# A fused transformer block: low parts of turned attention results on GpSimd, ScalarE's statistics a slot later, two more residual blocks turned by DMA

## The chip, the cores and the metric

The kernel runs on one core of a Trainium2 chip. The core has five engines that each work through a list of instructions of their own: TensorE (PE; its weight loads are shown apart as PEld), VectorE (DVE), ScalarE (ACT), GpSimd (POOL) and SyncE (SP), which here only issues DMAs. The metric is the device time of one execution in microseconds (us). The kernel before takes 512.64 us, the median of three runs (511.61 to 512.82).

## What is computed

One pre-norm transformer block over 2048 tokens of 512 features: sliding, dilated attention (32 heads of 16 features, 8 keys per query, 2 tokens apart), then a layer with 1792 hidden units and a squared ReLU. All in float32.

```python
h  = x + attention(layernorm(x) @ wqkv) @ wo
h2 = h + relu(layernorm(h) @ w1 + b1)**2 @ w2 + b2
```

where, for each query position, the attention is

```python
idx    = pos[:, None] - arange(8) * 2
logits = einsum("bhsd,bhswd->bhsw", q, k[idx]) * scale      # masked where idx < 0
o      = einsum("bhsw,bhswd->bhsd", softmax(logits), v[idx])
```

## The kernel before

**Blocks and groups.** The 2048 tokens are 16 *blocks* of 128 tokens, t = 0 to 15, and four blocks make a *group* (group 0 is blocks 0 to 3, group 1 blocks 4 to 7 and so on). A block fills the 128 partitions.

**High and low parts.** TensorE multiplies in a shortened float32 (`F32R`). To keep the precision, each operand is split in two: the high part is a copy to that type, made on ScalarE (`hi`, L147), the low part is the operand less its high part, a subtraction on VectorE or GpSimd (`lo`, L150). A product is then three products: high by high, low by high, high by low (`mm3`, L232). Names ending in h and l are such parts: `oh` and `ol` of an attention result, `rh` and `rl` of a hidden unit's result, `big_l` (in one of its uses) of the turned residual.

**Stages.** First the products with wqkv (L232, tiles mm), group by group; their results go through memory (`qkv_d`), and the attention reads windows of them back. Then, for each group, the output product with wo (tiles wo), the norm, the first layer of the MLP (L232 again) and the second one (L870, tiles acc). The MLP of the first three groups (u = 0, 1, 2) runs while the blocks of the next group are prepared, and the products with wo of that next group stand in between. The last group's MLP has a schedule of its own (L793).

**Attention** runs beside all this on VectorE and GpSimd, as a stream of small steps: a product of q with a window of k (L343, pr<-qp,k), a reduction (L377, ex<-pr), a softmax over 8 keys, and a *weighing*, the product of the softmax with a window of v (L354, pr<-ex,v). The weighing is added up over the keys by three additions on GpSimd (L411: 256, 128 and 64 wide per row, here called one set of *sums*), the last of which writes the attention result o.

**Slots.** The order of all instructions is written by hand: the program goes through *slots* (one slot is one step of products on TensorE), and `at(n, ...)` puts a piece of work n slots on, `after(n, ...)` behind the attention steps of that slot. At the end of a slot the `at` pieces are issued, then `pump` issues as many attention steps as a running count of VectorE's time allows (`now["dve"]`, advanced by `dve(...)`, against TensorE's `now["pe"]`), then the `after` pieces. So a piece that no longer counts for VectorE also lets attention steps be issued earlier. Engines take what is issued to them in that order; buffers and results are guarded by semaphores.

**A block on its way from attention to the MLP.** The result o of a block has to be turned (features onto partitions) before the product with wo; so has the normed residual hn before the MLP. Either TensorE does it (four transposes, L205, into a tile tr), or a DMA: blocks 4, 5, 8, 9, 12 and 13 (the tables `OV` and `HV`) are turned by DMA. Then `o_split` copies o into two planes of 16 bits on ScalarE (L594, pl<-o), `turn_dma` issues a transposing DMA on SP (L598), and two slots after the split `o_join` puts the planes together again on ScalarE (L603), makes the high part oh (L147) and, at the end of that slot, the low part ol (`lo_T`, L150, on VectorE). The product with wo (`wo_product`) follows at the start of the next slot. For these six blocks its order is wo_h by oh, wo_l by oh, and last wo_h by ol (`lows_last`), four instructions each.

When the product is done, `h_add` (L639) adds the residual on VectorE: h<-wo,h. It then takes the statistics of the norm: for blocks 4, 5, 8, 9, 12 and 13 (`AS`) on ScalarE (`act_stats`, L181 to L183, tiles scrap, nm and sq), for the others on VectorE. GpSimd finishes them (L187 to L190), `h_norm` (L200) applies them on ScalarE, and hn is turned like o.

```python
        hi_T(tr, [oT[t][0]])
        after(0, lo_T, tr, [oT[t][0]], [oT[t][1]])
```

(o_join's last two lines: the high part on ScalarE, then the low part.)

Of the kernel before, what the change touches and what calls it, by code (L numbers as in the profile page):

```python
# [19 lines left out]
R = 4  # L20
RI = 2
# [9 lines left out]
LAG = 3  # L31
AS = (4, 5, 8, 9, 12, 13)
OV = (4, 5, 8, 9, 12, 13)
HV = (4, 5, 8, 9, 12, 13)
SLOW = 1.01, 1.10, 1.06
DELAY = 3
WJ = 2
# [1 line left out]
OT = 4, 5, 10, 12  # L39
WO = 7, 9, 13, 15  # L40
HT = 20, 20, 21, 23
OK = (-6, -2, 4), (-5, -1, 5), (3, 6, 10), (4, 7, 12)
HK = (12, 15, 18), (14, 16, 19)
W2 = (18,)
LH = 3, 4, 10, 11
OP = 6, 7, 12, 13
# [12 lines left out]
def block_kernel(ctx, tc, x, wqkv, wo, w1, b1, w2, b2, out):  # L59
# [52 lines left out]
    def at(delta, fn, *a):  # L112
        due.setdefault(now["slot"] + delta, []).append((fn, a))

    def after(delta, fn, *a):
        late.setdefault(now["slot"] + delta, []).append((fn, a))
# [14 lines left out]
    def dve(t):  # L131
        now["dve"] += t
# [16 lines left out]
    def lo(eng, dst, src, h):  # L149
        eng.tensor_tensor(out=dst, in0=src, in1=h, op=ALU.subtract)  # L150
# [63 lines left out]
        for d, src in parts(tr, h_dst):  # L214
            hi(d, src)

    def lo_T(tr, h_dst, l_dst):
        for (d, src), h in zip(parts(tr, l_dst), h_dst):
            lo(nc.vector, d, src, h)
            dve(0.16 + 0.53 / len(h_dst))  # L220

    def mm3(ps, lh, ll, rh, rl, mid=None, at_=2 * KB, lows_last=False):

# [346 lines left out]
    def o_T(t):  # L570
        s, j = divmod(t, RI)
        pump(until=s)
        tr = transposes(o_t[s][:, j, :])
        if t % R == RI:

            ohl = att.tile([P, 2, KB, P], F32R, name="ohl", tag="o", bufs=3)
            oT[t] = ohl[:, 0], ohl[:, 1]
        else:
            oT[t] = row("oh", (P, KB, P), F32R), row("ol", (P, KB, P), F32R)
        at(0, hi_T, tr, [oT[t][0]])  # L580
        at(0, lo_T, tr, [oT[t][0]], [oT[t][1]])
# [30 lines left out]
    def o_join(t):  # L612
        turn_join(("o", t))
        tr = planes.pop(("o", t))
        if t % R == RI:
            ohl = att.tile([P, 2, KB, P], F32R, name="ohl", tag="o", bufs=3)
            oT[t] = ohl[:, 0], ohl[:, 1]
        else:
            oT[t] = row("oh", (P, KB, P), F32R), row("ol", (P, KB, P), F32R)
        hi_T(tr, [oT[t][0]])  # L620
        after(0, lo_T, tr, [oT[t][0]], [oT[t][1]])

    def h_split(t):
        turn_split(("h", t), hn.pop(t))
# [12 lines left out]
    def h_add(t, ps):  # L637
        h = hs[t]
        nc.vector.tensor_tensor(out=h, in0=ps, in1=h, op=ALU.add)  # L639
        dve(0.7)  # L640
        (act_stats if t in AS else norm_stats)(t, h)

    def h_norm(t):
        hn[t] = row("hn")
# [13 lines left out]
    def wo_product(t, slots):  # L658
        ps = turn["mm"].tile("wo")
        oh, ol = oT.pop(t)  # L660
        mm3(ps, lambda k: oh[:, k, :], lambda k: ol[:, k, :],
            lambda k: wo_h[:, k, :], lambda k: wo_l[:, k, :], lows_last=t in OV)
        for n, (fn, a) in zip(slots, ((h_add, (t, ps)), (h_norm, (t,)), (add_b2, (t,)),
                                      (spill, (t,)))):
            (after if fn in (h_norm, spill) else at)(n + (fn is add_b2), fn, *a)

# [311 lines left out]
    def first_phase(t0):  # L980
        def chores(m):
            if t0 + 3 < 16:
                if m in (0, 2):
                    at(0, x_stats, t0 + 2 + m // 2)

                early = t0 == 12
                if m + early in (6, 7):
                    at(0, x_norm, t0 - 4 + m + early)
                if m in XT[early]:
                    x_T(t0 + 2 + XT[early].index(m))  # L990
            if t0 + 5 < 16 and m in (6, 9):
                at(0, load_x, t0 + 2 + m // 3)
            if jobs and m % 3 == 0:
                at(0, weight_job)
            k = t0 // 2 * 12 - 72 + m
            if k == 19:
                dve(HOLD)
            for t in range(R):
                if k == OT[t]:
                    at(0, load_h, t)  # L1000
                    if t not in OV:
                        o_T(t)
                if t in OV and k in OK[t]:
                    at(0, (o_split, lambda t: turn_dma(("o", t)), o_join)[OK[t].index(k)], t)
                if t in HV and k in HK[t]:
                    at(0, (h_split, lambda t: turn_dma(("h", t)),
                           lambda t: turn_join(("h", t)))[HK[t].index(k)], t)
                if k == WO[t]:
                    wo_product(t, (1, 3, 4, 6))
                    now["pe"] += 2.73  # L1010
                if k == HT[t]:
                    (at(0, h_parts, t) if t in HV else h_T(t))
            if k in W2:
                at(0, load_w2, W2.index(k))

        def half(m):
            end_slot(1.37)
            chores(m)

        for n in range(6):  # L1020
            chores(2 * n)
            qkv_of(t0 + n % 2, n // 2, lambda: half(2 * n + 1))
            end_slot(1.37)
# [41 lines left out]
    for u in range(R - 1):  # L1065
        now["sub"] = u
        first, end = u == 0, False
        fs = list(range(FB)) if first else [*sorted(place), 12, 13]
        fs += [f for f in range(12) if f not in fs and (u < 2 or f not in ENDS)]
        fs += ENDS if u == 2 else []  # L1070
        need = [] if first else [f for f in fs if f < 12 and f not in place]
        acc = [psum.tile([P, D], F32, name="acc", tag=tag) for tag in ("acc0", "acc1", "tr0", "tr1")]
        js = range(R)


        todo, halves = {}, {}
        for i in js:
            t = R * (u + 1) + i
            if not end:
                a = i // 2 if u == 2 else 0  # L1080
                o0 = OP[i] - a
                if t in OV:
                    turned = [(o0, at, 0, o_split, t), (o0, after, 0, turn_dma, ("o", t)),
                              (o0 + 2, at, 0, o_join, t)]
                else:
                    turned = [(o0, o_T, t)]
                if t in HV:
                    h0 = 12
                    turned += [(h0, at, 0, h_split, t), (h0, after, 0, turn_dma, ("h", t)),
                               (h0 + 2, at, 0, turn_join, ("h", t))]  # L1090
                for p, *what in ((LH[i] - a, at, 0, load_h, t), *turned,
                                 (WP[i] - a, wo_product, t, (0, 1, 2 + 3 * a, 3 + 3 * a))):
                    todo.setdefault(p, []).append(what)
                p, h = (HP[i], i % 2) if u < 2 else HL[i]
                if t in HV:
                    todo.setdefault(p, []).append((at, 0, h_parts, t))
                else:
                    (todo, halves)[h].setdefault(p, []).append((h_T, t))
            todo.setdefault(UP[i], []).append((at, 0, unspill, R * u + i))
        if u == 2:  # L1100
            for p, *what in ((12, at, 0, t_load, 0), (12, at, 0, t_load, 1), (13, after, 0, t_sums, 0),
                             (13, after, 0, t_sums, 1), (13, at, 1, t_split, 0),
                             (14, after, 0, t_split, 1)):
                todo.setdefault(p, []).append(what)

        def half(p):
            run(due)
            for fn, *a in halves[p]:
                fn(*a)

        for p in range(FB + LAG):
            more = 0.0
            if p == FB:
                run(due)
                dve(HOLD)
            if u < 2 and p == FB - 2:
                dve(HOLD)
            for fn, *a in sorted(todo.get(p, []), key=lambda x: x[0] is wo_product):
                fn(*a)
                more += 2.73 if fn is wo_product else 0.0  # L1120
            if p < FB:
                mlp1(u, fs[p])
                more += 2.73
                if first:
                    at(0, split_w2, p)
                    if p + 1 < FB:
                        load_w2(p + 1)
            q = p - LAG
            if q >= 0:
                f = fs[q]  # L1130
                mlp2(u, f, acc, js, q == 0, q == FB - 1,
                     (lambda: half(p)) if p in halves else None)
                more += 2.74
                if f < 12 and (need or first and p < FB - LAG):
                    free.append(place.pop(f))
                    if need:
                        at(1, fetch, need.pop(0))
            end_slot(more)
        for i in js:
            at(u // 2, finish, R * u + i, acc[i])  # L1140
# [83 lines left out]
```

## Time and profile before

| what | value |
|---|---|
| median of 3 runs | 512.64 us (511.61 to 512.82) |
| the profiled execution | 512.31 us, of which span 510.5 us |
| granted TensorE clock, mean | 0.999 |

The span is the time from the first to the last instruction. Busy time of the engines by stretch, from the view by windows (us):

| stretch | PE | DVE | ACT | POOL | what runs |
|---|---|---|---|---|---|
| 0 to 64 | 60.10 | 45.91 | 31.71 | 34.32 | start, products with wqkv of group 0 |
| 64 to 160 | 96.00 | 87.94 | 59.70 | 77.34 | products with wqkv, wo of group 0 |
| 160 to 260 | 100.00 | 87.32 | 62.82 | 76.34 | MLP of group 0, wo of group 1 |
| 260 to 360 | 98.83 | 87.48 | 54.62 | 78.43 | MLP of group 1, wo of group 2 |
| 360 to 430 | 70.00 | 32.92 | 40.64 | 48.74 | MLP of group 2, wo of group 3 |
| 430 to 510.5 | 76.92 | 35.16 | 41.40 | 36.08 | MLP of group 3 |

In the rows of the profile that follow, a group of instructions reads: line, engine, operation, tile written <- tiles read, shape, count | busy time, mean ns of one | idle time of the engine before them, and what ended it. A row of a timeline begins with the start and the duration in us, and ends, where the engine stood idle, with that idle time and what ended it. Rows of the chain of waits have start, duration, engine and tile.

### The profile page before, as it was taken

The numbers are of one execution on the slowest core, as the hardware profiler recorded it, in microseconds if no ns is written. First come the engines' busy times: TensorE is split into PE (matmuls) and PEld (weight loads), VectorE is DVE, ScalarE is ACT, GpSimd is POOL, SyncE is SP. The second block draws the span as 40 slices with busy tenths as digits, with TensorE's granted clock in tenths as the row PEclk, the third lists the DMA queues.
The fourth block names the chain that finished last, engine by engine and source line by source line (L and its number), as shares of the span: only waits on it lengthen the run. The fifth ranks groups of instructions, "written<-read, shape, count | busy, mean of one in ns | idle before, by whom it ended". The sixth has DMA issues, their size and how long they took to land. (4 is left out here: it accounts for less than half of the span.)

```text
span 510.5 us, 7598 instructions
## 1 busy us (share of the span) xinstructions
PE 501.9 (98%) x2460; PEld 424.4 (83%) x2460; DVE 376.7 (74%) x512; ACT 290.9 (57%) x552; POOL 351.2 (69%) x430
## 2 busy tenths in 40 slices
PE   7999999999999999999999999999999999999997
PEld 6999788888888888888888878888888888998986
DVE  5479899988998899788879979899963046832233
ACT  4634686767434767485364557264564737666541
POOL 4714799895786798786778768776897364685610
PEclk9999999999999999999999999999999999999999
DMA  8678998989677889666587955767672172444112
GB/s 264 180 225 203 256 295 299 271 285 274 204 225 214 276 301 272 200 199 174 182 253 217 226 166 163 202 199 249 207 152 67 52 217 84 160 142 133 62 42 83
DMA packets 100912, 100.52 MB, mean 197 GB/s; under 512 B 21000, under 2 KB 69384, under 8 KB 100872
## 3 DMA queue, kind: packets, MB, share of 16 engines
q1 hardware_dynamic: 99928, 99.52, 65.4%
q10 hardware_dynamic: 944, 0.52, 0.3%
q8 instruction: 19, 0.31, 0.3%
q14 instruction: 21, 0.17, 0.1%
HBM read 72.65 MB, written 24.25 MB: 190 GB/s over the span
## 5 line engine op out<-in xcount | busy, mean ns | idle before, releaser
L411 POOL TENSOR_TENSOR pr<-pr 128x512 f32<-128x512 f32 (+1 forms) x128 | 132.5, 1035 | 45.7 <-DVE pr L354 40.3
L232 PE MATMUL mm<-big_l,w_h 128*128 128x512 f32 x336 | 88.7, 390 | 0.0
L354 DVE TENSOR_TENSOR pr<-ex,v 128x1024 f32<-128x1024 f32 x64 | 78.2, 1222 | 12.8 <-POOL o L411 6.5
L343 DVE TENSOR_TENSOR pr<-qp,k 128x1024 f32<-128x1024 f32 x64 | 76.9, 1202 | 5.6 <-ACT qp L272 5.5
L377 DVE TENSOR_REDUCE ex<-pr 128x64 f32<-128x1024 f32 x64 | 78.4, 1226 | 1.9
L232 PEld LDWEIGHTS mm<-big_l,w_h 128*128 128x128 f32 x336 | 62.8, 188 | 13.0
L150 POOL TENSOR_TENSOR rl<-r,rh 128x512 fp32r<-128x512 f32 x42 | 56.2, 1339 | 19.6 <-ACT rh L147 16.5
L232 PE MATMUL mm<-big_h,xl 128*128 128x512 f32 (+1 forms) x208 | 56.0, 379 | 0.2 <-DVE xl L150 0.2
L232 PE MATMUL mm<-big_h,xh 128*128 128x512 f32 (+1 forms) x208 | 53.5, 378 | 0.7 <-ACT xh L147 0.7
L232 PE MATMUL mm<-big_l,xh 128*128 128x512 f32 (+1 forms) x208 | 52.8, 375 | 0.0
L870 PE MATMUL acc<-big_l,rh 128*128 128x512 f32 x190 | 52.2, 390 | 0.0
L870 PE MATMUL acc<-big_h,rh 128*128 128x512 f32 x190 | 52.1, 391 | 0.0
L501 ACT COPY y<-mm 128x512 f32<-128x512 f32 (+1 forms) x52 | 28.6, 552 | 41.2 <-PE mm L232 33.0
L870 PE MATMUL acc<-big_h,rl 128*128 128x512 f32 x190 | 51.7, 389 | 0.0
L846 ACT ACTIVATE r<-mm,b_sb 128x512 f32<-128x512 f32 x42 | 28.8, 685 | 32.4 <-PE mm L232 32.3
L232 PE MATMUL mm<-big_l,w_l 128*128 128x512 f32 x168 | 45.0, 389 | 0.0
L232 PEld LDWEIGHTS mm<-big_h,xh 128*128 128x128 f32 x208 | 37.6, 188 | 7.0 <-ACT xh L147 1.5
L232 PEld LDWEIGHTS mm<-big_l,xh 128*128 128x128 f32 x208 | 38.2, 188 | 6.1 <-POOL big_l L150 0.2
L232 PEld LDWEIGHTS mm<-big_h,xl 128*128 128x128 f32 x208 | 37.2, 188 | 5.8 <-DVE xl L150 0.6
L870 PEld LDWEIGHTS acc<-big_h,rl 128*128 128x128 f32 x190 | 35.7, 188 | 7.5
L870 PEld LDWEIGHTS acc<-big_l,rh 128*128 128x128 f32 x190 | 35.5, 188 | 7.4
L870 PEld LDWEIGHTS acc<-big_h,rh 128*128 128x128 f32 x190 | 34.9, 188 | 6.7
(160 smaller groups left out, 904.1 us busy)
## 6 DMA issues: line engine op xcount, KB each, us to landing
k<-qkv_d SPq DMA_DIRECT2D x48, 288.0 KB, 2.8
v<-qkv_d SPq DMA_DIRECT2D x48, 288.0 KB, 3.2
qkv_d<-y SPq DMA_DIRECT2D x18, 512.0 KB, 4.2
big_l<-w2l_d SPq DMA_DIRECT2D x24, 256.0 KB, 3.0
xt<-in_A_x_dram SPq DMA_DIRECT2D x16, 256.0 KB, 4.6
q<-qkv_d SPq DMA_DIRECT2D x32, 128.0 KB, 4.7
h<-in_A_x_dram SPq DMA_DIRECT2D x16, 256.0 KB, 3.9
h_d<-h SPq DMA_DIRECT2D x16, 256.0 KB, 3.2
```

Source lines behind the costliest of these rows:

```text
L150: eng.tensor_tensor(out=dst, in0=src, in1=h, op=ALU.subtract)
L232: nc.tensor.matmul(ps, l(k), r(k), start=(n == 0), stop=(n == 3 * KB - 1))
L343: nc.vector.tensor_tensor(out=pr.rearrange("p i w h d -> p i w (h d)"), in0=qps["now"][:, j % 2].unsqueeze(2).to_broadcast([P, RI, W, GC]) ...
L354: nc.vector.tensor_tensor(out=p2, in1=vwin, op=ALU.mult, in0=e1[:, :, :, j * GH:(j + 1) * GH].unsqueeze(4).to_broadcast([P, RI, W, GH, DH]))
L377: nc.vector.tensor_reduce(out=lf[:, :, :, j * GH:(j + 1) * GH], in_=pr, axis=X, op=ALU.add)
L411: nc.gpsimd.tensor_tensor(out=dst, in0=p2[:, :, :w], in1=p2[:, :, w:2 * w], op=ALU.add)
L501: nc.scalar.copy(y[:, :, t % RI * GC:(t % RI + 1) * GC], ps[:, :j * GC].rearrange("p (j c) -> p j c", j=j))
L846: nc.scalar.activation(r, ps, AF.Relu, bias=b1_sb[:, f:f + 1])
L870: nc.tensor.matmul(acc[j], l[:, j * P:(j + 1) * P], w[f], start=(first and n < len(js)), stop=(last and n >= len(terms) - len(js)))
```

## The change

Four edits, in one diff:

1. `act_stats` is issued one slot after `h_add` instead of in its slot, and `h_norm` of those blocks follows at the slot after that, ahead of the attention steps instead of behind the ones of the slot before.
2. The low part ol of a block turned by DMA is made by GpSimd instead of VectorE, with no time counted for VectorE. For blocks 12 and 13 it is issued ahead of the slot's attention steps instead of behind them.
3. Blocks 0 and 1 join `HV`: their normed residual is turned by DMA in the stage of the products with wqkv (split at step 12 or 14 of its count, join at 18 or 19), and not by TensorE at step 20.
4. The table entries for turning o in group 0 by DMA go away (`OK`; no block of group 0 was in `OV`). The new terms in `o0` and `turned` apply to blocks with `i >= RI`, and no such block is in `OV`, so they move nothing.

```diff
-HV = (4, 5, 8, 9, 12, 13)
+HV = (0, 1, 4, 5, 8, 9, 12, 13)
...
-OK = (-6, -2, 4), (-5, -1, 5), (3, 6, 10), (4, 7, 12)
-HK = (12, 15, 18), (14, 16, 19)
+HK = (12, 18), (14, 19)
...
-    def lo_T(tr, h_dst, l_dst):
+    def lo_T(tr, h_dst, l_dst, eng=nc.vector):
         for (d, src), h in zip(parts(tr, l_dst), h_dst):
-            lo(nc.vector, d, src, h)
-            dve(0.16 + 0.53 / len(h_dst))
+            lo(eng, d, src, h)
+            if eng is nc.vector:
+                dve(0.16 + 0.53 / len(h_dst))
...
         hi_T(tr, [oT[t][0]])
-        after(0, lo_T, tr, [oT[t][0]], [oT[t][1]])
+        (after if t < 3 * R else at)(0, lo_T, tr, [oT[t][0]], [oT[t][1]], nc.gpsimd)
...
         dve(0.7)
-        (act_stats if t in AS else norm_stats)(t, h)
+        if t in AS:
+            at(1, act_stats, t, h)
+        else:
+            norm_stats(t, h)
...
-            (after if fn in (h_norm, spill) else at)(n + (fn is add_b2), fn, *a)
+            more = fn is add_b2 or fn is h_norm and t in AS
+            (after if fn in (h_norm, spill) and not (fn is h_norm and t in AS) else at)(
+                n + more, fn, *a)
...
-                    if t not in OV:
-                        o_T(t)
-                if t in OV and k in OK[t]:
-                    at(0, (o_split, lambda t: turn_dma(("o", t)), o_join)[OK[t].index(k)], t)
-                if t in HV and k in HK[t]:
-                    at(0, (h_split, lambda t: turn_dma(("h", t)),
-                           lambda t: turn_join(("h", t)))[HK[t].index(k)], t)
+                    o_T(t)
+                if t in HV and k == HK[t][0]:
+                    at(0, h_split, t)
+                    after(0, turn_dma, ("h", t))
+                if t in HV and k == HK[t][1]:
+                    at(0, turn_join, ("h", t))
...
-                o0 = OP[i] - a
+                o0 = OP[i] - a - (2 if i >= RI and t in OV else 0)
                 if t in OV:
-                    turned = [(o0, at, 0, o_split, t), (o0, after, 0, turn_dma, ("o", t)),
+                    turned = [(o0, at, 0, o_split, t), (o0, at if i >= RI else after, i // RI, turn_dma, ("o", t)),
                               (o0 + 2, at, 0, o_join, t)]
```

How the built order moves, at three places. The numbers behind the names are the program's own and differ a little between the two builds; no time is in these rows.

VectorE around h_add of block 4 (h_2101 before, h_2095 now), before:

```order
L354 TENSOR_TENSOR pr_2390<-ex_226,v_2234 128x1024
L377 TENSOR_REDUCE ex_226<-pr_2343 128x16x4
L343 TENSOR_TENSOR pr_2400<-qp_2398,k_2336 128x1024
L354 TENSOR_TENSOR pr_2406<-ex_226,v_2284 128x1024
L150 TENSOR_TENSOR ol_2385<-pl_2271,oh_2384 128x512
L150 TENSOR_TENSOR big_l_85<-raw2_2306,big_h_84 128x512
L639 TENSOR_TENSOR h_2101<-wo_2412,h_2101 128x512
L377 TENSOR_REDUCE ex_226<-pr_2400 128x16x4
```

and now:

```order
L354 TENSOR_TENSOR pr_2388<-ex_226,v_2271 128x1024
L377 TENSOR_REDUCE ex_226<-pr_2341 128x16x4
L343 TENSOR_TENSOR pr_2398<-qp_2396,k_2334 128x1024
L149 TENSOR_TENSOR big_l_85<-raw2_2299,big_h_84 128x512
L639 TENSOR_TENSOR h_2095<-wo_2406,h_2095 128x512
L354 TENSOR_TENSOR pr_2460<-ex_226,v_2282 128x1024
L377 TENSOR_REDUCE ex_226<-pr_2398 128x16x4
L343 TENSOR_TENSOR pr_2468<-qp_2396,k_2343 128x1024
L354 TENSOR_TENSOR pr_2472<-ex_226,v_2390 128x1024
```

The low part is gone from VectorE, and the weighing that stood ahead of h_add (pr_2406) now stands behind it (pr_2460).

GpSimd between the low parts of blocks 4 and 5, before (neither is here):

```order
L411 TENSOR_TENSOR pr_2390<-pr_2390 128x2x256
L411 TENSOR_TENSOR pr_2390<-pr_2390 128x2x128
L411 TENSOR_TENSOR o_2113<-pr_2390 128x2x64
L150 TENSOR_TENSOR rl_2454<-r_2452,rh_2453 128x512
L411 TENSOR_TENSOR pr_2406<-pr_2406 128x2x256
L411 TENSOR_TENSOR pr_2406<-pr_2406 128x2x128
L411 TENSOR_TENSOR o_2113<-pr_2406 128x2x64
L411 TENSOR_TENSOR pr_2481<-pr_2481 128x2x256
```

and now, with ol_2383 of block 4 and ol_2455 of block 5:

```order
L411 TENSOR_TENSOR o_2111<-pr_2388 128x2x64
L149 TENSOR_TENSOR ol_2383<-pl_2265,oh_2382 128x512
L149 TENSOR_TENSOR rl_2448<-r_2446,rh_2447 128x512
L411 TENSOR_TENSOR pr_2460<-pr_2460 128x2x256
L411 TENSOR_TENSOR pr_2460<-pr_2460 128x2x128
L411 TENSOR_TENSOR o_2111<-pr_2460 128x2x64
L411 TENSOR_TENSOR pr_2472<-pr_2472 128x2x256
L411 TENSOR_TENSOR pr_2472<-pr_2472 128x2x128
L411 TENSOR_TENSOR o_2111<-pr_2472 128x2x64
L149 TENSOR_TENSOR ol_2455<-pl_2320,oh_2454 128x512
```

Each low part stands behind the sums of its slot; between the two are the sums of two weighings, pr_2460 and pr_2472, both issued by VectorE behind h_add of block 4. Blocks 8 and 9 read the same way.

GpSimd at the end of the attention, by blocks 12 and 13, before:

```order
L411 TENSOR_TENSOR pr_4197<-pr_4197 128x2x256
L411 TENSOR_TENSOR pr_4197<-pr_4197 128x2x128
L411 TENSOR_TENSOR o_3988<-pr_4197 128x2x64
L150 TENSOR_TENSOR rl_4235<-r_4233,rh_4234 128x512
L411 TENSOR_TENSOR pr_4202<-pr_4202 128x2x256
L411 TENSOR_TENSOR pr_4202<-pr_4202 128x2x128
L411 TENSOR_TENSOR o_3988<-pr_4202 128x2x64
L150 TENSOR_TENSOR rl_4288<-r_4286,rh_4287 128x512
```

and now:

```order
L411 TENSOR_TENSOR o_3986<-pr_4195 128x2x64
L411 TENSOR_TENSOR pr_4200<-pr_4200 128x2x256
L411 TENSOR_TENSOR pr_4200<-pr_4200 128x2x128
L411 TENSOR_TENSOR o_3986<-pr_4200 128x2x64
L149 TENSOR_TENSOR rl_4236<-r_4234,rh_4235 128x512
L149 TENSOR_TENSOR ol_4242<-pl_4127,oh_4241 128x512
L149 TENSOR_TENSOR rl_4286<-r_4284,rh_4285 128x512
L149 TENSOR_TENSOR ol_4292<-pl_4185,oh_4291 128x512
```

The last set of sums has moved ahead of rl, and the two low parts, of blocks 12 and 13, stand behind it, one rl apart.

## The prediction

> **What bounds the kernel now.** I read the page's first part, then TensorE's list of waits, then the chain of waits, and last the timelines around each place that the change touches.
>
> ```profile
> PE 501.9 (98%) x2460; PEld 424.4 (83%) x2460; DVE 376.7 (74%) x512; ACT 290.9 (57%) x552; POOL 351.2 (69%) x430
> PE wo L232 <- DVE ol L150: 1.2, 2, 0.6
> ```
>
> TensorE is busy for 98% of the span. The second row is the only wait in its list that isn't for an operand of the input x or of the warm-up: twice, 0.6 us each, a product with wo waits for a low part ol. So a change can win little (fewer TensorE instructions, and these 1.2 us), while any input that comes late is paid in full. The chain of waits shows where those two stand:
>
> ```profile
> 294.91 0.90 DVE ol L150
> 295.86 1.21 PE wo L232 x4
> 304.17 0.67 DVE ol L150
> 304.88 1.21 PE wo L232 x4
> 306.10 2.75 PE mm L232 x12
> 317.01 0.44 PE tr L205 x4
> ```
>
> Ahead of 305 us the chain comes through VectorE and GpSimd into ol (blocks 8 and 9), and from there it stays on TensorE for more than 100 us. The low part of a turned block is thus the one place where these engines meet with no slack, and the change moves just that operation from VectorE to GpSimd.
>
> **Durations.** Means from the page, and the present low part from the view of tile ol:
>
> ```profile
> L354 DVE TENSOR_TENSOR pr<-ex,v 128x1024 f32<-128x1024 f32 x64 | 78.2, 1222 | 12.8 <-POOL o L411 6.5
> L343 DVE TENSOR_TENSOR pr<-qp,k 128x1024 f32<-128x1024 f32 x64 | 76.9, 1202 | 5.6 <-ACT qp L272 5.5
> L377 DVE TENSOR_REDUCE ex<-pr 128x64 f32<-128x1024 f32 x64 | 78.4, 1226 | 1.9
> L150 POOL TENSOR_TENSOR rl<-r,rh 128x512 fp32r<-128x512 f32 x42 | 56.2, 1339 | 19.6 <-ACT rh L147 16.5
> L150 DVE TENSOR_TENSOR ol<-pl,oh x6: 683/812/1017, 203.0 to 387.6; 128x512 fp32r<-128x512 f32 x6
> ```
>
> No ol runs on GpSimd yet. Its nearest row there is rl, the same subtraction of the same shape: 1.34 us mean, 1.74 us where it was slowest below. I take 1.3 us. The skill weighs in here: the Trainium skill, GPSIMD Engine Reference, opens by calling GpSimd the wrong engine for plain elementwise work, with VectorE roughly twice as fast. The rows say 1.34 against 0.81 us, a ratio of 1.6; by the page's 2 an ol would take an estimated 1.6 us, and each of the three or four stalls below would grow by 0.3 us, to some 520.5 us in all. I keep the row's value.
>
> **Two blocks of group 0 turned by DMA.** Eight transposes leave TensorE. The chain prices four at 0.44 us, so 0.9 us is saved. In exchange ScalarE gets four copies and SP two transposing DMAs.
>
> ```profile
> L594 ACT COPY pl<-hn x6: 1040/1042/1042, 226.1 to 406.6; 128x1024 uint16<-128x1024 uint16 x6
> L603 ACT COPY pl<-hn x6: 1160/1164/1171, 240.2 to 424.4; 128x1024 uint16<-128x1024 uint16 x6
> DMA to landing us min/median/max: 4.3/4.7/5.1
> 145.33 0.59 ACT L501 COPY y<-mm 128x512 f32<-128x512 f32 x1 [3.38 <-PE mm L232]
> 150.82 0.59 ACT L501 COPY y<-mm 128x512 f32<-128x512 f32 x1 [4.31 <-PE mm L232]
> ```
>
> That is 2 x (1.04 + 1.16) = 4.4 us on ScalarE, against 3.4 and 4.3 us in which it sat idle in just those slots. A DMA has five or six slots (five slots are about 14 us) for 4.7 us until the join. The loads of v, k and q that follow on SP's queue may start some tenths later; no row shows TensorE waiting for one. Cost: nothing while these idles last, 0.5 us at most if the evacuation y slips behind a copy. I take -0.9 us; bounds -1.0 and -0.4.
>
> **Statistics on ScalarE a slot later.** Six blocks, three small activations each, are issued behind the next slot's evacuation instead of ahead of it.
>
> ```profile
> 306.86 0.63 ACT L181 ACTIVATE scrap<-h 128x512 f32<-128x512 f32 x1 [4.96 <-DVE h L639]
> PE mm L232 <- ACT xh L147: 0.7, 1, 0.7
> PE tr L205 <- ACT xt L200: 0.4, 1, 0.4
> ```
>
> ScalarE now stands up to 5.0 us there, waiting for h. TensorE waits for ScalarE just twice, for parts of the input, and never for anything of the groups' stages, so the freed time is worth nothing: 0. The norm, its turn at slot 12 and the join at 14 keep their slots. Were that cover gone, the first to be late would be the turned residual parts at the group's end; I put 0 to 0.3 us there.
>
> **Low parts on GpSimd: the cost.** The order shown with the change tells what stands in front of each ol now: on GpSimd the sums of a weighing (L411), and behind them, for blocks 5 and 9, a second set whose product VectorE issues only behind h_add of the block before. That h_add waits for TensorE. So a ring closes: product of block 4, h_add, weighings, sums, ol, product of block 5.
>
> Blocks 4 and 5:
>
> ```profile
> 202.28 0.46 POOL L411 TENSOR_TENSOR o<-pr 128x128 f32<-128x128 f32 x1
> 205.92 1.07 PE L232 MATMUL wo<-wo_h,ol 128*128 128x512 f32 x4
> 207.03 0.69 DVE L639 TENSOR_TENSOR h<-wo,h 128x512 f32<-128x512 f32 x1 [2.70 <-PE wo L232]
> 211.19 2.44 POOL L411 TENSOR_TENSOR pr<-pr 128x512 f32<-128x512 f32 x2 [3.10 <-DVE pr L354]
> 213.71 0.79 POOL L411 TENSOR_TENSOR o<-pr 128x128 f32<-128x128 f32 x1
> 214.08 1.07 PE L232 MATMUL wo<-wo_h,ol 128*128 128x512 f32 x4
> ```
>
> Block 4: GpSimd is free at 202.74, ol ends at 204.0, TensorE wants it at 205.92. No wait. Block 5: h_add ends at 207.72. Then VectorE owes weighing 1.22, reduction 1.23, product 1.20 and weighing 1.22, to 212.6. A set of sums takes 2.66 us from its start (298.99) to its end (301.65, rows below), to 215.3; ol to 216.6. TensorE wants it at 214.08: **+2.5 us**. Bounds: 2.3, since the rows of VectorE overlap by 0.1 us; 3.5 if the sums are stretched as they were here at 211.19 (3.3 us).
>
> Blocks 8 and 9:
>
> ```profile
> 294.79 0.46 POOL L411 TENSOR_TENSOR o<-pr 128x128 f32<-128x128 f32 x1
> 295.21 1.74 POOL L150 TENSOR_TENSOR rl<-r,rh 128x512 fp32r<-128x512 f32 x1
> 297.09 0.69 DVE L639 TENSOR_TENSOR h<-wo,h 128x512 f32<-128x512 f32 x1 [1.29 <-PE wo L232]
> 298.99 2.12 POOL L411 TENSOR_TENSOR pr<-pr 128x512 f32<-128x512 f32 x2 [2.04 <-DVE pr L354]
> 301.18 0.47 POOL L411 TENSOR_TENSOR o<-pr 128x128 f32<-128x128 f32 x1
> 301.68 1.22 DVE L354 TENSOR_TENSOR pr<-ex,v 128x1024 f32<-128x1024 f32 x1 [0.39 <-POOL o L411]
> ```
>
> Block 8: ol starts at 295.25 in place of rl and ends at 296.55, where VectorE's ended at 295.81: **+0.75** (0.5 to 1.2, the latter with rl's 1.74 us). Block 9: h_add then ends at 297.78 + 0.75 = 298.53. Weighing 1.22, sums 2.66, the next weighing 1.22 (it waited for those sums, last row), sums 2.66, ol 1.3, and 0.3 us of gaps: 307.9, where the chain had TensorE start at 304.88. That is 3.0, less the 0.75 counted already: **+2.2** (1.5 to 3.3).
>
> Block 12:
>
> ```profile
> 382.55 2.11 POOL L411 TENSOR_TENSOR pr<-pr 128x512 f32<-128x512 f32 x2
> 384.74 0.79 POOL L411 TENSOR_TENSOR o<-pr 128x128 f32<-128x128 f32 x1
> 385.49 1.28 POOL L150 TENSOR_TENSOR rl<-r,rh 128x512 fp32r<-128x512 f32 x1
> 385.84 1.07 PE L232 MATMUL wo<-wo_h,ol 128*128 128x512 f32 x4
> 345.68 2.47 DVE L878 TENSOR_TENSOR h<-acc,h 128x512 f32<-128x512 f32 x4
> ```
>
> GpSimd has a backlog here. The sums that begin at 382.55 end at 385.2 undisturbed; the last sums, which now stand ahead of rl, at 387.9; rl at 389.2; ol at 390.5. TensorE wants it at 385.84: 4.7 us late, if the attention stream runs as it did. But the new order puts one weighing ahead of the four adds of 345.68 (2.47 us) and one ahead of h_add of block 9 (1.22 us), so the stream can be up to 3.7 us earlier, which leaves 1.0. I take a gain of 2.1, a little over half, so **+2.6** (1.0 to 4.7). Block 13's ol follows 2.6 us later, 8 us ahead of its use: 0.
>
> The sum: -0.9 + 0 + 2.5 + 0.75 + 2.2 + 2.6 = +7.15 us, bounds +4 and +12. The profiled execution took 512.31 us (510.5 of it span); it lies 0.33 below the median of 512.64. 512.31 + 7.15 = **519.5 us**. The 5 us that ol takes from VectorE gain nothing beyond this: VectorE waits for TensorE at each h_add anyway.
>
> **Rivals.** First, *the stalls pay for one another* (513.8 us). While TensorE stands 2.5 us at block 5, VectorE and GpSimd run ahead and later low parts come in time: 512.31 - 0.9 + 2.4. For it: they owe TensorE nothing in that time. Against it: VectorE's rows at 207.03 and 297.09 wait for TensorE's own product, so the lead is given back at each h_add.
>
> Second, *faster* (510.2 us). With ol gone from VectorE the weighings move up, GpSimd's idle times (3.10 us ahead of 211.19, 2.04 ahead of 298.99) take the subtraction, and the 1.2 us of waits vanish with the 0.9: 512.31 - 2.1. It decides at block 5: ol must land by 214.1, for which its weighings would have to stand ahead of h_add. Against it, the built order has one behind.
>
> Third, *the clock* (521.0 us). A stall could cost more than its length, if TensorE then ran slower for a while:
>
> ```profile
> 1.34 4.18 PE L918 MATMUL tr<-ident 128*128 128x128 f32 x24 [1.34 <-POOL mhalf L904]
> 0.00:4.00 4.00, 2.65 (x13) 2.66 (x14) 0.00 (x0) 1.28 (x1) 0.73 (x7) 1.00 0.55 132
> ```
>
> The first 24 transposes took 4.18 us, where 24 at 0.11 make 2.6: 1.5 us for one slow start, added once to 519.5. The granted clock reads 1.00 in that stretch, which speaks against a drop, and no stall so far was over 1.3 us. The Trainium skill, TensorE: Matmul & The Clock Gate, Part 1, says that an idle window of about 3.4 us halves the clock until a busy one has passed; by that rule only block 12's stall at its upper bound would trip it.
>
> **How the numbers follow.** 0.71 for the forecast (516 to 524), 0.12 for stalls that pay for one another, 0.09 for the clock, 0.08 for faster. A measurement of this kernel tells about 0.3% from no change, 1.5 us, so 511.1 to 514.2 counts as same. Faster 0.08; same 0.10, which is most of the first rival; slower 0.82. The range goes from 513.6, to take in the first rival, to 523.8; outside are the faster case and the top of the bounds.
>
> **What would show it.** TensorE's waits should name GpSimd's ol, at blocks 5, 9 and 12 with 2 us or more each, one below 1 at block 8, and none at 4 and 13. VectorE should stand some 4 us ahead of block 4's h_add. tr<-hn should count eight fewer with no new wait near 156 us. I am wrong in mechanism if TensorE doesn't wait for GpSimd, wrong in size if block 12 waits under 1 us or near 5, and wrong about the first two edits if it waits for ScalarE or for a turned residual part.

## The result, and the profile after

| | kernel before | changed kernel |
|---|---|---|
| median | 512.31 us (511.61 to 512.82, 4 runs) | 537.88 us (537.13 to 542.05, 4 runs) |
| ratio of the times | | 1.0517, 95% interval 1.0461 to 1.0573 |
| the profiled execution, span | 510.5 us | 536.5 us |
| granted TensorE clock, mean | 0.999 | 0.987 |

The changed kernel is 5.2% slower. The direction was forecast, but the time lies 18 us above the forecast and 14 us above the top of its range. TensorE's list of waits of the changed kernel (tile that was to be used, who released it; total us, times, longest us) shows what was foreseen and what was not:

```profile
PE wo L232 <- POOL ol L149: 10.4, 5, 3.5
PE mm L232 <- ACT r L851: 8.9, 2, 4.8
PE tr L204 <- ACT hn L199: 1.2, 1, 1.2
PE mm L232 <- ACT y L501: 0.7, 1, 0.7
```

The first row is the forecast: products with wo that wait for GpSimd's low part ol. The second row was in no part of it: twice, a product of the MLP's first layer waits more than 4 us for r, which is what ScalarE writes when it empties the bank of an earlier product of that layer. There is a third loss, which no list of waits can show. It is in TensorE's timeline of the changed kernel, around the long waits (start, duration, in brackets the idle time before and who ended it):

```profile
206.49 1.19 PE L232 MATMUL wo<-wo_h,ol 128*128 128x512 f32 x4 [0.61 <-POOL ol L149]
217.37 1.19 PE L232 MATMUL wo<-wo_h,ol 128*128 128x512 f32 x4 [2.42 <-POOL ol L149]
...
234.01 2.08 PE L232 MATMUL mm<-big_l,w_h 128*128 128x512 f32 x4 [4.11 <-ACT r L851]
...
239.12 1.07 PE L875 MATMUL acc<-big_l,rh 128*128 128x512 f32 x4
...
305.48 1.19 PE L232 MATMUL wo<-wo_h,ol 128*128 128x512 f32 x4 [1.29 <-POOL ol L149]
316.51 1.21 PE L232 MATMUL wo<-wo_h,ol 128*128 128x512 f32 x4 [2.58 <-POOL ol L149]
...
320.31 1.07 PE L875 MATMUL acc<-big_h,rh 128*128 128x512 f32 x4
...
333.93 2.07 PE L232 MATMUL mm<-big_l,w_h 128*128 128x512 f32 x4 [4.84 <-ACT r L851]
335.80 1.91 PE L232 MATMUL mm<-big_l,w_l 128*128 128x512 f32 x4
...
340.20 1.07 PE L875 MATMUL acc<-big_l,rh 128*128 128x512 f32 x4
...
410.18 1.38 PE L232 MATMUL wo<-wo_h,ol 128*128 128x512 f32 x4 [3.48 <-POOL ol L149]
...
415.55 0.84 PE L875 MATMUL acc<-big_h,rh 128*128 128x512 f32 x3
```

Four groups of four products take 3.80 us at full speed: 316.51 to 320.31, behind an idle time of 2.58 us. Behind the idle times of 4.11, 4.84 and 3.48 us the same four groups take 5.11, 6.27 and 5.37 us (234.01 to 239.12, 333.93 to 340.20, 410.18 to 415.55). So TensorE did not only stand; when it went on it was slow for a while, which cost 1.31 + 2.47 + 1.57 = 5.4 us. The granted clock says the same (view by windows; it is the number ahead of the last two, which are the DMA engines' busy share and rate):

```profile
330.00:336.00 6.00, 2.08 (x5) 1.69 (x6) 0.00 (x0) 3.45 (x5) 4.07 (x7) 0.71 0.31 100
336.00:342.00 6.00, 6.00 (x20) 4.71 (x20) 4.18 (x4) 3.50 (x6) 1.84 (x3) 0.72 0.25 55
```

It is 0.71 and 0.72 in these two stretches of 6 us. The parts together:

| part of the 26.0 us of span | us |
|---|---|
| waits for ol, 10.4 where 1.2 was | +9.2 |
| waits for r | +8.9 |
| waits for hn and y | +1.9 |
| slow TensorE after three waits | +5.4 |
| eight transposes fewer | -0.9 |
| sum | 24.5 |

1.5 us are in none of these rows. (The wait for hn is also in the run without edit 1 below and in none of the runs of one edit alone; what makes it stays open.)

**Why r is late.** The timeline of ScalarE and GpSimd ahead of block 5's r and the product behind it (slot 12 of the MLP of group 0). In the kernel before:

```profile
220.74 0.19 POOL L190 TENSOR_TENSOR rs<-nm,rs 128x1 f32<-128x1 f32 x1
...
223.47 0.81 ACT L200 ACTIVATE hn<-h,rs 128x512 f32<-128x512 f32 x1
224.19 0.67 ACT L846 ACTIVATE r<-mm,b_sb 128x512 f32<-128x512 f32 x1
```

and in the changed kernel, from block 4's hn on to the product at 234.01:

```profile
224.38 0.82 ACT L199 ACTIVATE hn<-h,rs 128x512 f32<-128x512 f32 x1 [2.75 <-POOL rs L189]
225.10 0.67 ACT L851 ACTIVATE r<-mm,b_sb 128x512 f32<-128x512 f32 x1
...
226.99 0.63 ACT L180 ACTIVATE scrap<-h 128x512 f32<-128x512 f32 x1
...
228.42 2.09 POOL L411 TENSOR_TENSOR pr<-pr 128x512 f32<-128x512 f32 x2
...
232.35 0.19 POOL L189 TENSOR_TENSOR rs<-nm,rs 128x1 f32<-128x1 f32 x1
...
232.57 0.81 ACT L199 ACTIVATE hn<-h,rs 128x512 f32<-128x512 f32 x1 [3.00 <-POOL rs L189]
233.29 0.67 ACT L851 ACTIVATE r<-mm,b_sb 128x512 f32<-128x512 f32 x1
```

Already in the kernel before, hn stands directly ahead of r on ScalarE, but its rs had been ready for 2.5 us (since 220.93), so neither waited. The first edit leaves hn ahead of the same r and puts the statistics behind the r of the slot before. Now hn of block 4 waits 2.75 us for rs, and r behind it with it. From r come rh and rl; GpSimd's rl and sums then stand ahead of block 5's rs, the statistics of block 5 (226.99) stand behind that r on ScalarE, and hn of block 5 waits 3.00 us in its turn. The r behind that one empties the bank of slot 11's product. In slot 12 one of the two banks for mm holds the transposes of block 6's attention result (o_T), so the product of slot 12 can't start before r has emptied the other. (The use of the two banks is read from the code; the waits are measured.)

### The profile page after: what moved, and what is told of

Read it like the earlier page. It is cut to its first block, busy times and chain, and to the rows that moved or that the text cites. A ratio compares the mean times of both kernels' runs of the same rounds, so it can differ in the third digit from the quotient of the medians.

```text
span 536.5 us, 7581 instructions
## 1 busy us (share of the span) xinstructions
PE 508.4 (95%) x2452; PEld 427.7 (80%) x2452; DVE 373.3 (70%) x506; ACT 294.5 (55%) x556; POOL 357.4 (67%) x436
## 5 line engine op out<-in xcount | busy, mean ns | idle before, releaser
L232 PE MATMUL mm<-big_l,w_h 128*128 128x512 f32 x336 | 92.3, 402 | 9.6 <-ACT r L851 8.9
L232 PEld LDWEIGHTS mm<-big_l,w_h 128*128 128x128 f32 x336 | 64.9, 194 | 24.2 <-ACT r L851 9.4
L149 POOL TENSOR_TENSOR rl<-r,rh 128x512 fp32r<-128x512 f32 x42 | 54.3, 1294 | 34.0 <-ACT rh L146 28.7
L232 PE MATMUL mm<-big_l,w_l 128*128 128x512 f32 x168 | 46.9, 403 | 0.0
```

The source lines that it names most:

```text
L232: nc.tensor.matmul(ps, l(k), r(k), start=(n == 0), stop=(n == 3 * KB - 1))
```

## The experiments

"Edit 1, 2, 3" are those of the section on the change.

**Edit 1 alone.**

```diff
-        (act_stats if t in AS else norm_stats)(t, h)
+        if t in AS:
+            at(1, act_stats, t, h)
+        else:
+            norm_stats(t, h)
...
-            (after if fn in (h_norm, spill) else at)(n + (fn is add_b2), fn, *a)
+            more = fn is add_b2 or fn is h_norm and t in AS
+            (after if fn in (h_norm, spill) and not (fn is h_norm and t in AS) else at)(
+                n + more, fn, *a)
```

> The kernel before with only the statistics on ScalarE a slot later. Theory A: the order itself makes ScalarE wait. h_norm of block 5 (and 9) stands ahead of the evacuation r of slot 12, and its statistics now come so late that r frees TensorE's bank late: two waits of TensorE for ACT r of 3 to 5 us each, the clock drops behind them, 520 to 528 us. Rival B: those waits are an echo of the stalls for ol on GpSimd, which push h_add and the sums back: alone this edit costs nothing, 512 us +- 1.5, and no wait for ACT r.

Measured: 524.12 us, 12.0 above the 512.08 us of the kernel before, measured beside it (ratio 1.0235, 1.0217 to 1.0252). From its list of waits and from TensorE's timeline:

```profile
PE mm L232 <- ACT r L851: 7.9, 2, 4.1
```

```profile
230.46 1.29 PE L232 MATMUL mm<-big_l,w_h 128*128 128x512 f32 x4 [4.12 <-ACT r L851]
...
327.05 2.07 PE L232 MATMUL mm<-big_l,w_h 128*128 128x512 f32 x4 [3.79 <-ACT r L851]
```

The waits for r come with edit 1 and need neither of the others; the waits for ol are those of the kernel before (1.2 us). So the edit priced at nothing costs, alone, almost half as much as the whole change.

**Edit 2 alone.**

```diff
-        after(0, lo_T, tr, [oT[t][0]], [oT[t][1]])
+        (after if t < 3 * R else at)(0, lo_T, tr, [oT[t][0]], [oT[t][1]], nc.gpsimd)
```

(and `lo_T` counts no VectorE time on GpSimd, as in the change)

> The kernel before with only the low parts of DMA-turned attention results on GpSimd. Theory A: TensorE's waits for POOL ol as in the changed kernel, 8 to 11 us in all (0.5 to 1.5 us at blocks 4 and 8, 2 to 3 at 5 and 9, about 3 at 12), no long wait for ACT r: 521 to 525 us. Rival B: the waits for ACT r come along with these, 530 us or more.

Measured: 522.2 us, +10.1 (ratio 1.0202, 1.0182 to 1.0222). Its list of waits has

```profile
PE wo L233 <- POOL ol L150: 7.9, 3, 3.4
```

and one wait of 1.1 us for r. Two of the three waits for ol, of 3.43 us (block 9) and 3.25 us (block 12), are followed by slow products, which take 1.30 and 1.58 us more (worked out over four groups as above). The third, of 1.20 us, is at block 5; blocks 4 and 8 don't wait here, although they do in the changed kernel.

**Edit 3 alone.**

```diff
-HV = (4, 5, 8, 9, 12, 13)
+HV = (0, 1, 4, 5, 8, 9, 12, 13)
...
-HK = (12, 15, 18), (14, 16, 19)
+HK = (12, 18), (14, 19)
```

(with the lines of `first_phase` that use HK and OK, as in the change)

> The kernel before with only blocks 0 and 1 turned by DMA. Theory A: eight transposes less, 0.9 us, against a wait of about 0.7 us for ACT y at the end of group 0's stage: 511.5 to 513 us, not told from the kernel before. Rival: the DMAs and copies delay the attention stream and with it a later ol, over 514 us.

Measured: 516.98 us, +4.9 (ratio 1.0093, 1.0076 to 1.0111). My expectation fell: the edit that was to save 0.9 us costs 4.9. The loss is at block 9, some 140 us behind the edit, where TensorE waits 3.7 us for ol:

```profile
PE wo L231 <- DVE ol L149: 3.9, 2, 3.7
```

VectorE's timeline ahead of it, in the kernel before:

```profile
293.69 1.22 DVE L343 TENSOR_TENSOR pr<-qp,k 128x1024 f32<-128x1024 f32 x1
294.82 0.97 DVE L150 TENSOR_TENSOR ol<-pl,oh 128x512 fp32r<-128x512 f32 x1
297.09 0.69 DVE L639 TENSOR_TENSOR h<-wo,h 128x512 f32<-128x512 f32 x1 [1.29 <-PE wo L232]
```

and with edit 3:

```profile
297.51 0.69 DVE L638 TENSOR_TENSOR h<-wo,h 128x512 f32<-128x512 f32 x1 [1.89 <-PE wo L231]
300.40 1.22 DVE L342 TENSOR_TENSOR pr<-qp,k 128x1024 f32<-128x1024 f32 x1 [2.20 <-ACT qp L271]
...
306.64 1.76 DVE L149 TENSOR_TENSOR ol<-pl,oh 128x512 fp32r<-128x512 f32 x1
```

The product pr<-qp,k stood ahead of block 8's ol and h_add, and stands behind them now. There it waits 2.20 us for qp: on ScalarE the copy that makes qp has moved too, from 292.67 to 300.01, behind block 8's statistics (298.30 to 300.10), which need the same h_add. All that follows is late, and block 9's ol starts at 306.64. A slow stretch behind the wait takes another 1.57 us. Why did a product move that has nothing to do with blocks 0 and 1? The transposes that were removed also added 0.44 each to the running count of TensorE's time, `now["pe"]`; with 0.88 less in it, `pump` issues the attention steps later, for the rest of the program. That reading is tested further on.

**Edits 2 and 3, without edit 1.**

> The changed kernel without its edit of the statistics (low parts on GpSimd and blocks 0 and 1 turned by DMA). Theory A: no waits for ACT r, those for POOL ol as in the changed kernel: 520 to 525 us. Rival B: the waits for ACT r remain, since the stalls for ol cause them: 533 us or more.

Measured: 528.72 us, +16.6 (ratio 1.0323, 1.0289 to 1.0357). The list of waits has no row for r any more, and the row for ol is that of the changed kernel:

```profile
PE wo L232 <- POOL ol L149: 10.4, 5, 3.9
```

So the waits are as expected and the time is above what I expected: three waits (2.43, 2.58 and 3.86 us) were followed by slow products here, 5.6 us in all. The edits one by one cost 12.0 + 10.1 + 4.9 = 27.0 us, and 25.6 together. That these agree is in part chance, for the parts are not the same: edit 1 costs 12.0 us alone and 9.2 on top of the others (537.88 - 528.72), edit 3 costs 4.9 alone and 6.5 on top of edit 2 (528.72 - 522.2), and its wait for VectorE's ol at block 9 can't come up where GpSimd makes ol.

**The changed kernel with r first in its slot.**

```diff
-        at(1, hidden, u, f, ps)
+        due.setdefault(now["slot"] + 1, []).insert(0, (hidden, (u, f, ps)))
```

> The changed kernel with one edit: on ScalarE the evacuation r of the first MLP product is put first in its slot, ahead of hn and all else that is issued there. Theory A (the queue on ScalarE: r stands behind hn, which waits for GpSimd's rs, and TensorE needs r's bank): the two waits of TensorE for ACT r (4.11 and 4.84 us in the changed kernel) fall under 0.5 us each, the granted clock stays at 1.00 after the places where they stood, and the time falls by 8.9 us and by the two clock losses of about 1.7 us, to 523.5 to 527 us; the three waits for POOL ol (10.4 us) stay. Rival B (the statistics themselves come too late, whatever stands behind them): a wait of the same size comes up for a turned residual part or for hn, and the time stays over 533 us.

Measured: 532.23 us, 5.65 below the changed kernel. Its list of waits:

```profile
PE wo L232 <- POOL ol L149: 10.5, 5, 3.8
PE mm L232 <- DVE ol L149: 2.3, 2, 1.6
PE tr L204 <- DVE ohl L149: 1.8, 1, 1.8
```

The waits for r are gone, and no product is slow at those places. But the time falls by 5.65 us where theory A gave 11 to 14, since 4.1 us of new waits come up: on ScalarE the high part of block 6's attention result (ohl, 233.49) stands behind the late hn (230.89) and its split, and VectorE stands idle for it for 4.20 us.

Theory A holds for r, rival B for a part of the rest. By these rows the span should be 8.5 us shorter (-8.9 + 4.1 - 3.8 of slow products, 0.1 longer at ol); it is 6.9 shorter, and 1.6 us stay unexplained.

**Edit 1 alone, with r first.** The edits of the first run and of the last together.

> The kernel before with the first edit alone (statistics on ScalarE a slot later), and with r put first in its slot on ScalarE. Theory A (all that the first edit costs is that r stands behind hn): no wait for ACT r, no low clock, and of the 12.0 us of the first edit at most 2 are left: 512 to 514 us. Rival K (hn itself, a slot later and at the start of its slot, also holds up what is behind it on ScalarE beside r: oh and ohl, for which VectorE's low parts wait, and TensorE for them): two or three waits of 1 to 2 us for DVE ol or ohl come up near 235 to 240 and 330 us, as they did with r first in the changed kernel (3.3 us), and the time is 515 to 518 us.

Measured: 514.38 us, +2.2 over its 512.22 us (ratio 1.0046, 1.0028 to 1.0064). There is no wait for r and no wait of over 0.7 us in the stages of the groups; rival K's waits do not appear. Of the 12.0 us of edit 1, 9.8 go when r no longer stands behind hn. The other 2.2 us are a little more than the 2 that theory A allowed, and the list of waits shows only about 1 us of them, in pieces of 0.2 and 0.3. That the new waits of the run before need the late low parts of edit 2 beside edit 1 is likely by this, but was not tried alone.

**Fillers ahead of the late products.** In the changed kernel:

```diff
+FILL = {(0, 12): 18, (1, 12): 21}
...
+            for n in range(FILL.get((u, p), 0)):
+                rh, _ = hid[u, fs[p - LAG - 1]]
+                nc.tensor.matmul(acc[0], nil, w2_h[fs[0]], start=False, stop=False)
```

(`nil` is a tile of zeros)

> The changed kernel with products by a tile of zeros on TensorE, accumulated into the first accumulator (they add zero), issued just ahead of the first MLP product of slot 12: 18 of them in group 0's stage, 21 in group 1's. They fill the idle time before the two late products and move no data and no other work. Theory C (the granted clock drops after an idle time of over about 3 us, and it is this that costs the rest of the 26 us): the wait for ACT r falls under 2.5 us at both places with the fillers ahead of it, the granted clock is 1.00 in 230 to 242 and 330 to 342 us where it was 0.71 to 0.92, and the time falls by two times 1.7 us, to 533.5 to 535.5 us (more than nothing although TensorE does more work). Rival D (the clock drops for another reason, or the drop costs nothing on the path): the clock still drops there, and the time is unchanged or longer, 537 to 541 us.

Measured: 536.01 us, 1.9 below the changed kernel, between what theory C and rival D gave. TensorE's timeline:

```profile
217.17 1.75 PE L234 MATMUL wo<-wo_h,ol 128*128 128x512 f32 x4 [2.42 <-POOL ol L151]
...
231.06 4.36 PE L1130 MATMUL acc<-big_h,nil 128*128 128x512 f32 x18
235.25 1.07 PE L234 MATMUL mm<-big_l,w_h 128*128 128x512 f32 x4
```

```profile
316.32 1.87 PE L234 MATMUL wo<-wo_h,ol 128*128 128x512 f32 x4 [2.58 <-POOL ol L151]
...
330.21 5.05 PE L1130 MATMUL acc<-big_h,nil 128*128 128x512 f32 x21
335.10 1.07 PE L234 MATMUL mm<-big_l,w_h 128*128 128x512 f32 x4
```

Where TensorE was kept busy, the product behind runs at full speed (1.07 us where it was 2.08 and 2.07), although it starts no earlier in its stage. The granted clock is 1.00 from 230 to 242 and from 330 to 342 us, where it was 0.86 and 0.72. So the idle time makes the slowness, not the lateness: theory C. The gain is smaller than expected, because two other idle times, of 2.42 and 2.58 us, which had no consequence in the changed kernel, are followed by slow products in this execution, 1.57 us each.

**Edit 3 with the running count kept.**

```diff
                     (at(0, h_parts, t) if t in HV else h_T(t))
+                    now["pe"] += 0.44 if t < 2 else 0.0
```

(on top of edit 3 alone)

> The kernel before with only blocks 0 and 1 turned by DMA, as in the run that did this alone (516.98 us), and with 0.44 added to the running count of TensorE's time for each of the two blocks at the step where their transposes stood, so that the attention steps are issued in the slots where they were before. VectorE's order is then that of the kernel before, but for the tile that block 0's and 1's low parts are read from. Theory E (the 4.9 us of that run come from the moved attention steps, not from the two turns): the wait of 3.7 us for DVE ol is gone, the waits are those of the kernel before (1.2 us for ol), and the time is the 0.9 us of the eight transposes below it, 511 to 512 us. Rival F (the two turns themselves, their DMAs or ScalarE's four copies, hold attention's inputs or ol up): the time stays at 515 to 518 us with the wait for ol in its place.

Measured: 512.64 us against 512.04 (ratio 1.0007, 0.9997 to 1.0018). One line brings back 4.3 of the 4.9 us: theory E. The 0.9 us of the transposes are not seen, and the list of waits shows why:

```profile
PE wo L231 <- DVE ol L149: 2.2, 2, 1.7
```

1.0 us more than before is spent waiting for ol, and 0.7 us once for y. In this execution the load of q ahead of ol landed about 2 us later than in that of before (ScalarE's copy that waits for it starts at 294.79 instead of 292.67). Whether the two new DMAs do that was not settled.

**The same, with ol ahead of the attention steps, on VectorE.**

```diff
-        after(0, lo_T, tr, [oT[t][0]], [oT[t][1]])
+        at(0, lo_T, tr, [oT[t][0]], [oT[t][1]])
```

> The run before this one (two more blocks turned, attention steps in their old slots) and, beside it, ol left on VectorE but issued ahead of the running count's attention steps of its slot instead of behind them, which is the half of the second edit that does not name GpSimd. Theory G (the 1.2 us of TensorE's waits for DVE ol in the kernel before come from the steps ahead of it in its slot): no wait for ol over 0.2 us is left, and the time is 509.5 to 511 us, below the kernel before. Rival H (ol waits for oh on ScalarE, so its place in VectorE's queue sets nothing, and the attention steps behind it are late instead): the wait stays or another of 1 us takes its place, 511 to 513 us.

Measured: 510.86 us against 512.04 (ratio 0.9981, 0.9968 to 0.9993; 10 and 20 runs). The waits for wo's low part are gone from the list, and one of 0.4 us is left for another product:

```profile
PE mm L231 <- DVE ol L149: 0.4, 1, 0.4
```

Theory G, but for these 0.4 us, where 0.2 at most were expected. This kernel is the best of all here, 0.2% faster than the kernel before.

**Low parts on GpSimd, ahead of the attention steps.**

```diff
-            lo(nc.vector, d, src, h)
+            lo(eng, d, src, h)
...
-        after(0, lo_T, tr, [oT[t][0]], [oT[t][1]])
+        at(0, lo_T, tr, [oT[t][0]], [oT[t][1]], nc.gpsimd)
```

(the count for VectorE is charged as before)

> The kernel before with the low parts of the DMA-turned attention results on GpSimd, but issued ahead of the attention steps of their slot for all six blocks (the change does so for blocks 12 and 13 alone), and with the count for VectorE charged as before, so that the attention steps stay in their slots. Theory I (the waits for POOL ol come from its place behind the additions of halves on GpSimd): of the 7.9 us of waits for POOL ol in the run of the second edit alone under 3 us are left, and the time is 512 to 515 us. Rival J (GpSimd is still busy with the additions of earlier slots when oh is there, so the place in the slot sets nothing, or the 1.3 us of the operation against 0.7 us on VectorE do it): over 5 us of waits are left and the time is 518 us or more. Block 12, which is issued ahead of the sums in the change too, and still waited 3.25 us, speaks for the rival there.

Measured: 513.29 us against 512.22 (ratio 1.0018, 0.9988 to 1.0049). GpSimd by block 12, in the run of edit 2 alone:

```profile
388.88 2.10 POOL L412 TENSOR_TENSOR pr<-pr 128x512 f32<-128x512 f32 x2
391.07 0.45 POOL L412 TENSOR_TENSOR o<-pr 128x128 f32<-128x128 f32 x1
391.48 1.26 POOL L150 TENSOR_TENSOR rl<-r,rh 128x512 fp32r<-128x512 f32 x1
392.69 1.26 POOL L150 TENSOR_TENSOR ol<-pl,oh 128x512 fp32r<-128x512 f32 x1
```

and in this run:

```profile
383.03 1.28 POOL L150 TENSOR_TENSOR rl<-r,rh 128x512 fp32r<-128x512 f32 x1
384.26 1.26 POOL L150 TENSOR_TENSOR ol<-pl,oh 128x512 fp32r<-128x512 f32 x1
385.49 2.10 POOL L411 TENSOR_TENSOR pr<-pr 128x512 f32<-128x512 f32 x2
```

The same operation on the same engine, 1.26 us in both, but the last sums stand behind it and not ahead of it. 1.8 us of the 7.9 us of waits are left, at this block. Theory I: what edit 2 costs is the place of ol among the sums, not GpSimd's slower subtraction. The run changes two things that set this place, where ol is issued in its slot and the count, and how much each gives was not measured over all blocks. At block 12 it is the count: the run of edit 2 alone, too, issues ol ahead of its slot's attention steps there, and with the count charged the last sums stand behind rl again, as in the kernel before.

## Why the prediction was wrong in size

**What bounds the kernel: right, and too mild.** An input that comes late was to be "paid in full". It is paid in full and more: the slow products after three of the waits add 5.4 us.

**Low parts on GpSimd: right.** The total wait at each block (what was already waited for in the kernel before included):

| block | predicted | bounds | measured |
|---|---|---|---|
| 4 | 0 | | 0.61 |
| 5 | 2.5 | 2.3 to 3.5 | 2.42 |
| 8 | 0.75 + 0.6 | 1.1 to 1.8 | 1.29 |
| 9 | 2.2 + 0.6 | 2.1 to 3.9 | 2.58 |
| 12 | 2.6 | 1.0 to 4.7 | 3.48 |
| 13 | 0 | | 0 |

The sum is 10.4 where 9.25 was worked out, and block 4 waits where no wait was expected. The prediction read the order of all edits together, and it is for them together that the table holds: edit 2 alone waits 1.20 us at block 5, nothing at block 8, 3.43 at block 9 and 3.25 at block 12. The duration of one ol on GpSimd, from the view of tile ol of the changed kernel (min/median/max in ns):

```profile
L149 POOL TENSOR_TENSOR ol<-pl,oh x6: 1260/1266/1727, 204.7 to 411.3; 128x512 fp32r<-128x512 f32 x6
```

This is the 1.3 us taken from the row of rl, 1.6 times VectorE's 0.81. The Trainium skill, GPSIMD Engine Reference, has a ratio of about 2 in its opening; the row was nearer. The ring of product, h_add, weighings, sums and ol could be followed from the rows of before and the new order alone: from the end of block 8's h_add to the end of block 9's ol it takes 9.05 us (307.40 to 316.45), where 9.4 were worked out. A sign that failed is VectorE's lead at block 4's h_add: 2.42 us, not 4.

**Statistics a slot later: the step that failed.** The prediction said that TensorE "waits for ScalarE just twice, for parts of the input, and never for anything of the groups' stages, so the freed time is worth nothing: 0". This looks at what the edit frees and not at what it puts in front. The list of waits of the kernel before says that ScalarE's results came in time in the old order; it says nothing of an order in which the statistics stand behind r, so that rs comes late, hn waits for it, and the r behind hn waits too. I looked for the late consumer behind hn (the turned residual parts, "0 to 0.3 us") and not for what stands behind it in ScalarE's queue. The run of edit 1 alone measured 12.0 us for this term, where 0 was put, and r put first brought 9.8 of them back. The prediction did name the sign: it was to be "wrong about the first two edits if it waits for ScalarE". Of those two, the one on statistics was.

**Two blocks turned by DMA: the second step that failed.** "-0.9 us" was right for the eight transposes (tr<-hn counts 28 instead of 36), and y waits 0.7 us once, a little over the 0.5 allowed. But the prediction costed the work and not the count that the work carries in the planner: "Cost: nothing while these idles last". Alone the edit costs 4.9 us, 4.3 of which go with the 0.88 of the running count.

**The rivals.** *The stalls pay for one another* did not happen: the waits for ol stand side by side in the changed kernel as they were added up. *Faster* was to be decided at block 5, and block 5 waits 2.42 us. *The clock* was the right mechanism, at "1.5 us for one slow start" with nearly the right size (1.57 us in most cases), but counted once, on top of the forecast. The size was in part luck: it came from the first 24 transposes, where the granted clock reads 1.00, and no run shows that their slowness is the same thing. There were three, two of them behind the waits for r, which the forecast didn't have. By the rule of the Trainium skill, TensorE: Matmul & The Clock Gate, Part 1 (an idle window of about 3.4 us), the three idle times of 3.48 us and more are those that count in the changed kernel, and its trace agrees. The prediction held only block 12's upper bound against that rule; its upper bounds for blocks 5 and 9, 3.5 and 3.9 us of wait, lie above 3.4 as well.

**The range.** Its bounds, +4 to +12, summed the bounds of edit 2 with 0.3 us for edit 1 and -0.4 for edit 3 at most. The two edits whose cost the trace of before doesn't show had the narrowest bounds; 16.9 us came from them when each ran alone.

## What to carry to other kernels

When an instruction is issued later, list what waits for its result, and then what stands behind that waiter in its own engine's order and who needs it. Here the statistics moved, hn waited for them, and it was the r behind hn that TensorE needed. Where a planner places work by a running count, removing an operation also moves everything that is placed after it, so keep the count when only the operation is to be tried. And when waits are added up for an engine that was slow after idle times, as TensorE was here, add the slow time after each wait of 3 us or more, and count one of some 2.5 us as one that may cost it too.

## What the runs showed of the hardware

Over the profiles of the changed kernel and of all these runs, every one of eleven idle times of TensorE of 3.09 us or more in the stages of the groups was followed by slow products. Of eight idle times of 2.42 to 2.58 us, four were and four were not; the same two places ran on at full speed in the changed kernel and slowly in the run with fillers. None of 1.79 us or less was, and none between 1.79 and 2.42 us came up. A slow group of four products starts 1.71 us before the next (335.80 to 337.50 in the changed kernel), a fast one 0.91, so the speed is 0.53, and most slow stretches cost 1.57 us, which is 3.3 us of slow running. That length fits the busy window of about 3.4 us that the Trainium skill gives in TensorE: Matmul & The Clock Gate, Part 1. Its idle window of the same length does not fit as a limit: 2.42 or 2.43 us were enough in two of four executions. Nor does the drop always come while TensorE stands: in three of the fifteen slow stretches (one each in the runs of edit 2 alone, without edit 1, and with r first in the changed kernel) the first group behind the wait still started 1.03 or 1.04 us before the next, as at full speed, and the slow groups came behind it.
